# An RWKV attention block and a SwiGLU block in one kernel: weight checks moved to the result buffers, gates made due sooner, last stores on two queues

## The chip, the cores and the metric

The kernel runs on one core of a Trainium2 chip. The metric is the device time of one execution in microseconds. A core has five engines that work side by side and each take their own instructions in order: TensorE (PE, matrix products; PEld is its weight load), VectorE (DVE), ScalarE (ACT), GpSimd (POOL) and SyncE (SP), which here issues the DMA transfers. Engines wait for one another through semaphores.

## The reference

Two blocks follow each other, in float32, with the weights of the second given as float64.

```python
# attention: r, k, v are (B, H, S, D) = (4, 8, 768, 48)
for t in range(S):
    cur = einsum('bhd,bhe->bhde', u * k[t], v[t])
    y[t] = einsum('bhd,bhde->bhe', r[t], state + cur)
    state = w * state + einsum('bhd,bhe->bhde', k[t], v[t])
# bridge: y becomes x, 3072 tokens by 384
xn = x / sqrt(mean(x * x) + 1e-6) * rms_g
out = (silu(xn @ w_gate) * (xn @ w_val)) @ w_out      # 384 -> 1536 -> 384
```

## The kernel before

**Stages.** The sequence is cut into 12 chunks of 64 positions; one chunk of all four batches is 256 tokens. For each chunk, `mixing` (line 735) does the attention: decayed products of r and k (A), a masked diagonal, the outputs (Y), the squares of the outputs into the tile `sq` (line 679), a root mean square (r, sqrt), the scaled tokens xa and xb (a copy with the halves exchanged), and the new state (U, E). `move` is a DMA of some heads' rows.

**The second block.** Chunks 0 and 1 are done in the plain way: cells `g` (gate and value of one group of 128 hidden units) and `P` (output product). During these first 150 us the float64 weights arrive as raw words and are rounded to float32 by VectorE (`bits1`, `bits2`), ScalarE (`ulp`) and GpSimd (`sum`). From chunk 2 on, chunks are taken in pairs (2 and 3, 4 and 5, to 10 and 11), and the two-by-two product of two halves of the weights by two chunks is made with seven products in place of eight. `group` (line 1028) does this for one of six groups of hidden units: products f1 to f7 of twelve matmuls each in the PSUM banks a, b and c, the copy `m1` of bank a on ScalarE, sums g1, g2, g3 on VectorE, Silu on ScalarE (silu0, silu1, silu23), and the gated units h0, h1, h2, h3. f1 and f5 both go into bank a: m1 is copied between them, silu0 and h0 read it after f5. `second_layer` (line 1065) makes the output product of the pair in the same way: P1 to P7, four results (c11 in r0, c12 in r1, c21 in r2, c22 in r3), which lie in `rows_out` (line 313) and are stored by `result` (line 1090), two DMAs of 64 rows each. In the last pair P3, c12 and the store of r1 are split in two halves.

**The checks.** The rounding is exact only for weights whose magnitude is not tiny. `check` (line 713) looks at one of 36 parts of the weights: SP loads 384 KB of raw words from HBM, ScalarE takes Abs of their high words and then a Relu that counts into a column of `seen`. `some_checks` (line 729) adds five of them in the mixing of each chunk from chunk 2 on, until all are done; all use the place `sq`, one after the other. `flag` (line 1133) sums `seen` at the end, and every engine reads the one number `bad` into a register (line 1149); a general path in the program follows if it is not zero.

**What sets the order.** All this is recorded as operations of a `Plan` with an engine, an assumed cost, and keys that are read and written; keys give the dependences. `schedule` (line 128) gives each operation a due time, taken backwards from the goals of the TensorE operations along the dependences, and then lets each free engine take the ready operation that is due first. `search` (line 204) tries 2000 changes of the goals from each of four seeds for the stretch up to the first product of chunk 4. The instructions are then issued in the order of the planned starts, so each engine's order is fixed when the program is built. All of them carry the line 92 in the profile, that of the wrapper that issues them.

```python
for j, hop in self.then[i]:
    due = late[j] - by * (hop + cost)
    ...
    if due < late[i]:
        late[i] = due
```

A load's entry has its cost and `land`, the assumed time until its data can be read: `LAND` is 2.1.

Of the kernel before, what the change touches and what calls it, by code (L numbers as in the profile page):

```python
# [43 lines left out]
I64 = mybir.dt.int64  # L44
# [19 lines left out]
L = 64  # L64
# [30 lines left out]
class Plan:  # L95
# [3 lines left out]
    HOP = 0.2  # L99
    SWITCH = 0.15  # L100
    AHEAD = 30.0
    KEEP = 2.0

    def __init__(self):
        self.ops, self.then, self.last, self.readers = [], [], {}, {}

    def add(self, engine, cost, reads, writes, give, land=0.0, port=False, name="", rows=False):

# [19 lines left out]
    def schedule(self, goals, free, count, relaxed, patience=0.3):  # L128

        if len(self.then) < len(self.ops):
            self.then = [[] for _ in self.ops]
            for i, op in enumerate(self.ops):
                for d in op[2]:
                    self.then[d].append((i, self.hop(d, i)))
        late = [goals.get(i, 1e6 + i) for i in range(len(self.ops))]
        early = min(goals[i] for i in goals if i >= relaxed) - self.AHEAD
        for i in reversed(range(len(self.ops))):
            by, cost = 2 if i >= relaxed else 1, self.ops[i][1]  # L140
            for j, hop in self.then[i]:
                due = late[j] - by * (hop + cost)
                if i < relaxed <= j and due < early:
                    due = early
                if due < late[i]:
                    late[i] = due
        n, then = count, self.then
        free, port = dict(free), {"DVE": 0.0, "POOL": 0.0}
        missing, mode = [len(op[2]) for op in self.ops[0:n]], None
        at, ready, start, end = [0.0] * n, {e: set() for e in free}, [0.0] * n, [0.0] * n  # L150
        for i in range(n):
            if not missing[i]:
                ready[self.ops[i][0]].add(i)
        for _ in range(n):
            when, e = min((max(free[e], min(at[i] for i in ready[e])), e) for e in free if ready[e])
            turn = (lambda i: late[i] + self.KEEP * (self.ops[i][7] != mode)) if e == "PE" else late.__getitem__
            i = min((i for i in ready[e] if at[i] <= when), key=turn)
            sooner = [j for j in ready[e] if at[j] <= when + patience and turn(j) < turn(i) - 1]
            if sooner:
                i = min(sooner, key=turn)  # L160
            s = max(when, at[i])
            if e == "PE":
                s += self.SWITCH * (self.ops[i][7] != mode)
                mode = self.ops[i][7]
            if self.ops[i][5]:
                s = max(s, port["POOL" if e == "DVE" else "DVE"])
            ready[e].remove(i)
            start[i], end[i] = s, s + self.ops[i][1]
            free[e] = end[i]
            if self.ops[i][5]:  # L170
                port[e] = end[i]
            for j, hop in then[i]:
                if j < n:
                    at[j] = max(at[j], end[i] + hop)
                    missing[j] -= 1
                    if not missing[j]:
                        ready[self.ops[j][0]].add(j)
        return start
# [58 lines left out]
def fast(ctx, tc, chan, tok, vpad, wka, wkb, wot, cols, u_row, out, bad):  # L237
# [444 lines left out]
    rms = diag.rearrange("p h t -> p (h t)")  # L682
    ku = raws.tile([P, B, HP, L], FP32, name="ku")
    ms = c_tile([P, 2, 2], "ms")
    turn = {"at": 0, "gv": 0, "h": 0}

    def next_at():
        turn["at"] += 1
# [23 lines left out]

    def check(n, src, k):

        keys = ["sq0", "sq1"]
        raw = sq.bitcast(I64).rearrange("p i t -> p (i t)")[:, 0:CHECK]
        hi = raw.bitcast(I32).rearrange("p (n z) -> p n z", z=2)[:, :, 1].bitcast(FP32)
        add(
            "SP", 0.95, [], keys, lambda: sp.dma_start(out=raw, in_=src[:, k * CHECK : (k + 1) * CHECK]), land=LAND,
            name=f"look {n}",  # L720
        )
        add("ACT", 0.57, [], keys, lambda: act.activation(hi, hi, AF.Abs), name=f"look {n}")
        add(
            "ACT", 0.81, [], keys + ["seen"],
            lambda: act.activation(hi, hi, AF.Relu, scale=-(2.0**15), bias=1.0, accum_out=seen[:, n : n + 1]),
            name=f"look {n}",
        )

    def some_checks():

        for n, (src, k) in list(to_check)[0:5]:
            check(n, src, k)
        del to_check[0:5]

    def mixing(s):

# [107 lines left out]
        if brief:  # L844
            for n in (2, 1):
                add(
                    "DVE", 0.15 + 0.27 * n, ["sq1"], ["sq0"],
                    lambda n=n: dve.tensor_add(sq[:, 0:n], sq[:, 0:n], sq[:, n : 2 * n]), port=True, name=f"q {s}",
                )
            add(  # L850
                "PE", 0.45, ["sq0", "sq1"], [key],
                lambda bank=bank: pe.matmul(bank[:, 0:NT], ones, sq[:, 0], start=True, stop=True), name=f"r {s}",
            )
            some_checks()
            add(
                "ACT", 3.1, [key], ["diag"],
                lambda bank=bank: act.activation(rms, bank[:, 0:NT], AF.Sqrt, scale=1.0 / DM, bias=eps), name=f"sqrt {s}",
            )
            add("DVE", 1.75, [], ["diag"], lambda: dve.reciprocal(rms, rms), name=f"inv {s}")
            add("DVE", 0.95, ["diag", "yT0", "yT1"], [f"xa{x}"], lambda: scaled(s, rms, yT), port=True, name=f"x {s}")  # L860
        else:
            for half in range(2):
                add(
                    "PE", 0.9, [f"sq{half}"], [key], lambda bank=bank, half=half: mean_squares(bank, sq, half),
                    name=f"r {s}",
                )
            if quick:
                add("ACT", 0.3, [key], ["ms"], lambda bank=bank: root(bank, ms[:, 0]), name=f"sqrt {s}")
                add("DVE", 0.15, [], ["ms"], lambda: dve.reciprocal(ms[:, 0], ms[:, 0]), name=f"inv {s}")
            else:  # L870
                add(
                    "DVE", 0.15, [key], ["ms"],
                    lambda bank=bank: dve.tensor_scalar(
                        out=ms[:, 1], in0=bank[:, 2 * P : 2 * P + 2], scalar1=1.0 / DM, scalar2=EPS, op0=ALU.mult,
                        op1=ALU.add,
                    ), name=f"ms {s}",
                )
                add("POOL", 0.6, ["ms"], ["ms'"], lambda: power(ms[:, 0], ms[:, 1]), port=True, name=f"pow {s}")
                add("DVE", 0.35, ["ms'"], ["ms"], lambda: refine(ms[:, 0], ms[:, 1]), name=f"inv {s}")
            add("DVE", 0.4, ["ms"], ["diag"], lambda: on_diagonal(ms[:, 0], diag), port=True, name=f"diag {s}")  # L880
            add("PE", 0.45, ["diag"], [key], lambda bank=bank: spread(bank, diag), name=f"spread {s}")
            add("DVE", 1.0, [key, "yT0", "yT1"], [f"xa{x}"], lambda bank=bank: scaled(s, bank, yT), name=f"x {s}")
# [145 lines left out]
    def group(s, m):  # L1028
# [18 lines left out]
        mm(xs_b, a_keys, a, lambda: wb[i][:, o], lambda: xb[s], False, "f5")  # L1047
        add("ACT", 0.38, ["sums"] + a_keys, ["g0"], lambda: act.activation(late["gv"][:, 0, 0], a[:, 0, 0:NT], AF.Silu), name="silu0")
        add("DVE", 0.42, a_keys + ["g0"], [f"h{m}.0"], lambda: dve.tensor_mul(h[:, 0], a[:, 1, 0:NT], late["gv"][:, 0, 0]), name="h0")
        mm(["t4"], b_keys, b, lambda: wb[i + 2][:, o], lambda: t_of(4), False, "f6")  # L1050
        add("DVE", 0.69, b_keys + ["m1"], ["g2"], lambda: dve.tensor_add(late["gv"][:, :, 2], b[sl], late["m1"]), name="g2")
        add("ACT", 0.62, [], ["g2", "g3"], lambda: act.activation(late["gv"][:, 0, 2:4], late["gv"][:, 0, 2:4], AF.Silu), name="silu23")
# [12 lines left out]
    def second_layer(s):  # L1065
# [22 lines left out]
            line.append(add("PE", 0.325 * len(js) * len(ms), reads, [keys[t]], give, name=f"{name} {s}"))  # L1088

        def result(k, chunk, f, js=(0, 1)):  # L1090
            def give():
                for bl in range(2):
                    to = bass.AP(
                        tensor=out.tensor, offset=out.offset + ((2 * js[0] + bl) * S + chunk * L) * DM + f * HALF,
                        ap=[[DM, L], [2 * S * DM, len(js)], [1, HALF]],
                    )
                    sp.dma_start(out=to, in_=results[bl * L : (bl + 1) * L, k, js[0] : js[-1] + 1])

            add("SP", 1.2, [f"r{k}"], [], give, name="store")

        def plus(writes, reads, to, x, y, name):
            add("DVE", 0.55, reads, writes, lambda: dve.tensor_add(to, x, y() if callable(y) else y), name=name)
# [30 lines left out]
    def flag():  # L1133
# [20 lines left out]
            lambda: pe.matmul(bank[0:1, 0:1], wrong, ones[:, 0:1], start=True, stop=True), name="flag",  # L1154
        )
        add("DVE", 0.2, [key], ["bad"], lambda: dve.tensor_copy(bad, bank[0:1, 0:1]), name="flag")
        add("ACT", 0.6, ["bad"], [], load, name="flag")

    t_sum = lambda s, n, reads, writes: add(
        "DVE", 0.95, reads, writes, lambda: token_sum(s, n), port=True, name=f"t{n} {s}"  # L1160
# [1 line left out]
    for s in range(FIRST, NS, 2):  # L1162
# [4 lines left out]
        t_sum(s, 4, xs_b + ["t2"], ["t4"])  # L1167
        if s == FIRST:
            add("DVE", 1.25, ["wa1.0", "wa1.1"], ["wa3.0", "wa3.1"], lambda: unit_sum(3, 1), port=True, name="sum 3'")
        for m in range(NN // 2):  # L1170
            group(s, m)
        if s == FIRST:
# [495 lines left out]
```

## Time and profile before

| | |
|---|---|
| median of 8 runs | 634.09 us (631.68 to 637.39) |
| profiled execution | 633.27 us |
| its span, first to last instruction | 631.5 us |
| mean granted TensorE clock | 0.995 |
| TensorE busy | 608.9 us, 96% of the span |
| VectorE, ScalarE, GpSimd busy | 437.5, 354.8, 42.8 us |
| HBM read and written | 55.94 MB, 4.72 MB |

The profile is that of one execution. "PE bank_a <- DVE h: 5.0, 3, 2.0" in the list of waits reads: TensorE, before instructions that write bank_a, stood idle for 5.0 us in total, three times, at most 2.0 at once, until an instruction of VectorE that writes h ended. A row of the timeline has start and duration in us, engine, line, operation, what it writes and reads, shapes and a count; in brackets stands the idle time before it and what ended it. A "q" behind an engine's name means its sequencer, which issues DMAs. A window's row has, for each engine, its busy time and number of instructions in the stretch, then the granted clock of TensorE as a share, the share of the DMA engines and GB/s.

### The profile page before, as it was taken

What the parts mean: (1) busy time and instruction counts of PE and PEld (TensorE: products, weight loads), DVE (VectorE), ACT (ScalarE), POOL (GpSimd) and SP (SyncE); (2) the same over time, 40 slices, a digit from 0 to 9 for tenths busy, and PEclk for the clock granted to TensorE, in tenths of its full rate; (3) what the DMA queues carried; (4) which work ended last, traced back from release to release, by engine and by line L of the source; (5) the groups of instructions that cost most, each with busy time, mean ns of one, the idle gap of its engine ahead of it and who ended that gap; (6) DMA issues with size and microseconds to landing.
All of it is one profiled execution on the core that took longest, in us unless ns stands there. A gap on an engine that the chain in (4) does not pass through costs nothing.

```text
span 631.5 us, 15364 instructions
## 1 busy us (share of the span) xinstructions
PE 608.9 (96%) x6544; PEld 538.4 (85%) x6544; DVE 437.5 (69%) x621; ACT 354.8 (56%) x895; POOL 42.8 (7%) x41
## 2 busy tenths in 40 slices
PE   8979999999999999999999899999999989999994
PEld 8867787777788899888899788899888889988994
DVE  7788788887776896477785468695556866455631
ACT  6888578675388447538958438948222774212200
POOL 2245323100000000000000000000000000000000
PEclk9998999999999999999999999999999999999999
DMA  8686763305404414142523242332104011100001
GB/s 283 215 324 205 251 220 120 109 14 176 144 7 125 153 33 100 51 153 67 144 85 97 76 150 60 110 118 57 26 1 152 12 31 32 26 1 2 1 13 44
DMA packets 22782, 62.92 MB, mean 100 GB/s; under 512 B 3152, under 2 KB 10160, under 8 KB 21296
## 3 DMA queue, kind: packets, MB, share of 16 engines
q1 hardware_dynamic: 22704, 61.85, 31.8%
q8 instruction: 53, 0.87, 0.6%
q14 instruction: 25, 0.20, 0.1%
HBM read 55.94 MB, written 4.72 MB: 96 GB/s over the span
## 4 chain that ended last, share of the span: by engine, by line
PE 88%; DMA 4%; ACT 3%; DVE 2%; SPq 1%; issue 1%; ACTq 0%
PE bank_b L92 28%; PE bank_a L92 26%; PE bank_c L92 23%; PE at L92 10%; DMA sq<-in_wka_dram 1%; DMA sq<-in_wot_dram 1%; DMA TOK<-in_tok_dram 1%; ACT L92 1%; SPq L92 1%; DMA VS<-in_vpad_dram 1%; ACT VS L92 1%; ACT sq L92 1%; DVE h L92 1%; DVE rows_out L92 1%; ACT MO L92 0%
## 5 line engine op out<-in xcount | busy, mean ns | idle before, releaser
L92 DVE TENSOR_TENSOR gv<-bank_b,m 128x512 f32<-128x512 f32 x90 | 62.1, 690 | 66.8 <-PE bank_b L92 64.7
L92 PE MATMUL bank_b<-xa,wa 64*128 64x256 f32 x444 | 55.0, 380 | 0.0
L92 ACT ACTIVATE sq<-sq 128x384 f32<-128x384 f32 x72 | 40.2, 559 | 24.1 <-DMA sq<-in_wot_dram 9.8
L92 ACT ACTIVATE gv<-gv 128x512 f32<-128x512 f32 (+1 forms) x60 | 31.1, 522 | 38.9 <-DVE gv L92 38.7
L92 PE MATMUL bank_a<-xa,wa 64*128 64x256 f32 x396 | 49.5, 382 | 3.0 <-DVE h L92 3.0
L92 PE MATMUL bank_a<-wo,h 128*128 128x192 f32 (+1 forms) x264 | 49.4, 343 | 2.0 <-DVE h L92 2.0
L92 ACT ACTIVATE gv<-bank_a 128x256 f32<-128x256 f32 x30 | 11.5, 382 | 70.0 <-PE bank_a L92 69.7
L92 DVE TENSOR_TENSOR gv<-bank_c,gv 128x512 f32<-128x512 f32 x60 | 41.4, 690 | 12.3 <-PE bank_c L92 11.1
L92 PEld LDWEIGHTS bank_a<-wo,h 128*128 128x128 f32 x264 | 43.5, 190 | 6.2 <-DVE h L92 2.1
L92 PE MATMUL bank_a<-xb,wb 64*128 64x256 f32 x396 | 48.7, 378 | 0.0
L92 ACT ACTIVATE ME<-dmask,du 64x64 f32<-64x64 f32 x176 | 45.8, 331 | 4.0 <-DVE du L92 3.3
L92 PEld LDWEIGHTS bank_b<-xa,wa 64*128 64x128 f32 x444 | 42.1, 187 | 6.4 <-issue 1.4
L92 ACT ACTIVATE MO<-dmask,du 64x64 f32<-64x64 f32 x176 | 46.5, 337 | 1.1 <-DVE du L92 0.7
L92 PE MATMUL bank_b<-t,wb 64*128 64x256 f32 x360 | 44.7, 381 | 1.2 <-DVE gv L92 1.2
L92 PEld LDWEIGHTS bank_a<-xa,wa 64*128 64x128 f32 x396 | 37.2, 187 | 9.8 <-DVE h L92 3.8
L92 PE MATMUL bank_c<-t,s 64*128 64x256 f32 x360 | 44.1, 377 | 0.0
L92 PE MATMUL bank_b<-t,s 64*128 64x256 f32 x360 | 44.0, 377 | 0.0
L92 PE MATMUL bank_c<-xb,s 64*128 64x256 f32 x360 | 43.9, 376 | 0.0
L92 ACT COPY m<-bank_a 128x512 f32<-128x512 f32 (+1 forms) x35 | 19.9, 569 | 40.2 <-PE bank_a L92 37.7
L92 PEld LDWEIGHTS bank_a<-xb,wb 64*128 64x128 f32 x396 | 38.0, 187 | 5.0 <-issue 0.5
L92 PE MATMUL bank_b<-wo,h 128*128 128x192 f32 (+1 forms) x168 | 38.4, 385 | 2.6 <-DVE h L92 2.6
L92 PEld LDWEIGHTS bank_b<-t,wb 64*128 64x128 f32 x360 | 34.2, 187 | 5.7 <-DVE gv L92 1.6
(152 smaller groups left out, 1253.2 us busy)
## 6 DMA issues: line engine op xcount, KB each, us to landing
chan<-in_chan_dram SPq DMA_DIRECT2D x11, 1024.0 KB, 5.5
TOK<-in_tok_dram SPq DMA_DIRECT2D x11, 768.0 KB, 5.8
VS<-in_vpad_dram SPq DMA_DIRECT2D x24, 256.0 KB, 4.2
raw<-in_wot_dram SPq DMA_DIRECT2D x8, 576.0 KB, 5.3
sq<-in_wka_dram SPq DMA_DIRECT2D x12, 384.0 KB, 3.3
sq<-in_wkb_dram SPq DMA_DIRECT2D x12, 384.0 KB, 3.1
sq<-in_wot_dram SPq DMA_DIRECT2D x12, 384.0 KB, 3.2
out_dram<-rows_out SPq DMA_DIRECT2D x46, 96.0 KB, 2.3
```

What stands on the lines that cost most here:

```text
L92: return lambda *args, **kwargs: self.tc.keep_in_program_order(give(*args, **kwargs))
```

## The change

The checks use `rows_out` in place of `sq`, its two halves (r0 and r1, r2 and r3) in turn, and their loads are assumed to land in 2 x 2.1 us. They are added in front of the six groups of a pair, eight to a pair, instead of in the mixing. The operation that makes h0 of every group gets a due time 3 us sooner, which passes on to all that it depends on. In the last pair the stores of r2 and r3 are issued from ScalarE's queue. All stores write a key, `stored`, that the reading of the flag reads.

```diff
     AHEAD = 30.0
+    URGENT = 3
...
+            if i in self.urgent:
+                late[i] -= self.URGENT
...
     def check(n, src, k):
-        keys = ["sq0", "sq1"]
-        raw = sq.bitcast(I64).rearrange("p i t -> p (i t)")[:, 0:CHECK]
+        turn["look"] = 1 - turn["look"]
+        keys = [f"r{2 * turn['look'] + i}" for i in range(2)]
+        raw = rows_out[:, turn["look"]].bitcast(I64).rearrange("p j f -> p (j f)")[:, 0:CHECK]
...
-            "SP", 0.95, [], keys, lambda: sp.dma_start(out=raw, in_=src[:, k * CHECK : (k + 1) * CHECK]), land=LAND,
+            "SP", 0.95, [], keys, lambda: sp.dma_start(out=raw, in_=src[:, k * CHECK : (k + 1) * CHECK]), land=2 * LAND,
...
     def some_checks():
-        for n, (src, k) in list(to_check)[0:5]:
+        share = -(-len(parts) // (NS // 2 - 1))
+        for n, (src, k) in to_check[0:share]:
             check(n, src, k)
-        del to_check[0:5]
+        del to_check[0:share]
...
     def mixing(s):
-            some_checks()
...
     def group(s, m):
         add("DVE", 0.42, a_keys + ["g0"], [f"h{m}.0"], lambda: dve.tensor_mul(h[:, 0], a[:, 1, 0:NT], late["gv"][:, 0, 0]), name="h0")
+        if m >= 0:
+            p.urgent.add(len(p.ops) - 1)
...
         def result(k, chunk, f, js=(0, 1)):
+            queue, issue = ("ACT", act) if k > 1 and s + 2 == NS else ("SP", sp)
...
-                    sp.dma_start(out=to, in_=results[bl * L : (bl + 1) * L, k, js[0] : js[-1] + 1])
-            add("SP", 1.2, [f"r{k}"], [], give, name="store")
+                    issue.dma_start(out=to, in_=results[bl * L : (bl + 1) * L, k, js[0] : js[-1] + 1])
+            add(queue, 1.2, [f"r{k}"], ["stored"], give, name="store")
...
     def flag():
-        add("ACT", 0.6, ["bad"], [], load, name="flag")
+        add("ACT", 0.6, ["bad", "stored"], [], load, name="flag")
...
     for s in range(FIRST, NS, 2):
+        some_checks()
         for m in range(NN // 2):
             group(s, m)
```

More of the change, by code (lines that the diff above doesn't have):

```diff
@@ L101 @@
     AHEAD = 30.0
+    URGENT = 3
     KEEP = 2.0
     def __init__(self):
-        self.ops, self.then, self.last, self.readers = [], [], {}, {}
+        self.ops, self.then, self.last, self.readers, self.urgent = [], [], {}, {}, set()
     def add(self, engine, cost, reads, writes, give, land=0.0, port=False, name="", rows=False):
@@ L684, in fast @@
     ms = c_tile([P, 2, 2], "ms")
-    turn = {"at": 0, "gv": 0, "h": 0}
+    turn = {"at": 0, "gv": 0, "h": 0, "look": 0}
     def next_at():
```

## The prediction

> **What bounds the kernel now.** I read the page's busy shares first, then TensorE's own waits, and then went to the place of each wait.
>
> ```profile
> PE 608.9 (96%) x6544; PEld 538.4 (85%) x6544; DVE 437.5 (69%) x621; ACT 354.8 (56%) x895; POOL 42.8 (7%) x41
> PEclk9998999999999999999999999999999999999999
> ```
>
> TensorE is busy for 608.9 of 631.5 us. The change adds and removes no matmul, so all it can move is the 22.6 us in which TensorE stands still, the 0.2 us lost when it changes between row modes (1.50 against 1.29 us for one set of twelve matmuls in the chain), and the dips of its clock. The waits of TensorE over the whole run:
>
> ```profile
> PE bank_a L92 <- DVE h L92: 5.0, 3, 2.0
> PE bank_b L92 <- DVE h L92: 2.6, 1, 2.6
> PE bank_c L92 <- POOL wa L92: 2.3, 1, 2.3
> ...
> PE bank_b L92 <- DVE gv L92: 1.2, 1, 1.2
> ...
> PE bank_c L92 <- DVE bad L92: 0.8, 1, 0.8
> ```
>
> By time, the ends are: 2.27 at 33.7 (POOL's weight sum), 2.56 at 45.5 (first output product P 0 0 waits for h), 1.25 at 163.0, 0.98 at 257.5, 2.03 at 354.4, 2.00 at 508.4 (output product P1 of the pair at chunk 8 waits for the last h0), and 0.80 at 620.9. After the last matmul 7.6 us follow. In the windows around the two early waits the fields after the span are PE, PEld, DVE, ACT, POOL, then the granted clock:
>
> ```profile
> 33.60:36.00 2.40, 0.14 (x4) 0.08 (x2) 2.34 (x5) 2.36 (x5) 2.09 (x3) 1.00 0.51 92
> 45.40:48.00 2.60, 0.06 (x1) 0.01 (x1) 2.25 (x6) 2.58 (x5) 1.83 (x2) 1.00 0.97 307
> 48.50:51.70 3.20, 3.20 (x6) 1.66 (x5) 3.06 (x9) 3.20 (x11) 1.72 (x2) 0.50 0.75 253
> ```
>
> So the wait at 45.5 costs twice: after it the clock is 0.50 for 3.2 us, and P 0 0 takes 5.64 us (48.02 to 53.66) where the same twelve take 3.91 elsewhere. That is 1.73 more. Now ScalarE and the SP queue around 354:
>
> ```profile
> 352.97 1.14 ACT L92 ACTIVATE sq<-sq 128x384 f32<-128x384 f32 x2 [4.67 <-DMA sq<-in_wka_dram]
> 354.21 1.28 ACT L92 ACT_TABLE_LOAD   x1
> 355.51 0.38 ACT L92 ACTIVATE gv<-bank_a 128x256 f32<-128x256 f32 x1
> ```
>
> A weight check stands in ScalarE's order ahead of the Silu of the unit group. Its load was issued at 348.88, behind four stores on SP, and came late; ScalarE stood 4.67 us, then loaded its table, then made silu0, and only then could VectorE make h0, for which TensorE waited 2.03. The waits at 257.5 (ScalarE idle 1.46 for a check's load) and 163.0 (5.72 and 3.29) have the same form. Checks follow one another through one place, sq, so a late load is late for the next one too.
>
> **The change part by part.** The sum is made against the profiled execution, 633.27 us, which is 0.82 under the median of 634.09.
>
> *Checks.* 36 checks stay: 36 loads of 384 KB and 72 activations (0.56 each, plus 36 read-outs of 0.19), about 47 us of ScalarE before and after. In the changed order they stand in pairs inside the first four unit groups of each pair of chunks (8, 8, 8, 8, 4), with two places in turn, and the scheduler assumes 4.2 instead of 2.1 us from the load to ScalarE. The load itself:
>
> ```profile
> DMA to landing us min/median/max: 3.0/3.2/7.3
> ```
>
> What must fit is store, then check, then ScalarE. The places are now rows_out, so a check's load waits on SP until the stores of the results have landed (2.3 median), and SP's next store queues behind it. Let f1 of a pair's first group start at T, when P3 (3.90) ends. By VectorE's order c22 is done about 1.5 earlier; with two issues of 0.6 its store lands at about T+1.6, and the even check, issued then, at T+4.8. The store of r1 (c12, after P3) queues behind that issue, is issued to T+3.3 and lands at T+5.0; the odd check lands at T+8.2. ScalarE has the even check behind silu0, until about T+6.4, and then stands to T+8.2. It makes 1.31 us of check, 0.63 of silu23 and 0.42 of silu1 and is free for the next m1 at T+10.6. The next f1 ends at T+10.4 (eight products of 1.295), and f5 wants m1 (0.58) at T+11.7: the late load is covered, by 0.5. So the three waits, 4.26 together, go; I leave 1.0 for loads above the median. Ends: none left, or all 4.26 again.
>
> *h0 made due 3 us sooner.* In 25 of 30 groups f5 now stands third among TensorE's seven products, ahead of f4 and f3; before it was fifth in 22. h0 is then ready about two products (2.6 us) earlier, which covers the 1.28 table load. P1 at chunk 8 waited 2.00 because h0 of the last group came last on VectorE; I leave 0.2. What is late next is m1: f5 adds to the bank that m1 is copied from. The nearest rows are one undisturbed group:
>
> ```profile
> 549.72 1.46 PE L92 MATMUL bank_a<-xa,wa 64*128 64x256 f32 x12
> 551.02 1.46 PE L92 MATMUL bank_b<-t,s 64*128 64x256 f32 x12
> 551.29 0.58 ACT L92 COPY m<-bank_a 128x512 f32<-128x512 f32 x1 [0.21 <-PE bank_a L92]
> 552.31 1.46 PE L92 MATMUL bank_c<-t,s 64*128 64x256 f32 x12
> ```
>
> m1 ends at 551.87, and the third product starts at 552.31: 0.44 of room, of which a handover takes 0.07 (the last product starts at 621.69, 0.07 after c12 ended at 621.62). So f5 costs nothing where ScalarE is free. In the groups beside mixing ScalarE may hold m1 behind a diagonal (1.05 for four); there are about two such places per pair, and I charge 1.0 in all. Ends: 0, and 0.4 in each of 30 groups, 12 us.
>
> *The first 150 us.* The due times and the checks' new places change the searched order. P 0 0 now stands behind a gate group, with h made before: the 2.56 and the 1.73 of clock go. New narrow places: a gate group behind VectorE's weight rounding (one pair of bits rows is 1.47), and the first f1 of chunk 2, which has only a root product (about 0.6 with its mode change) between it and the product whose h it follows (1.11 from product to h in the group above), so 0.5. I charge 2.0 for all of these; ends 0 and 4.3, as much as goes. The wait at 33.7 stays. TensorE changes row mode 69 times instead of 65: four times 0.20, 0.8.
>
> [...] The 2.56 wait was followed by a clock of 0.50, while those of 2.27, 2.03 and 2.00 were not. [...]
>
> *Last stores.*
>
> ```profile
> 623.93 0.36 DVE L92 TENSOR_TENSOR rows_out<-bank_c,rows_out 128x192 f32<-128x192 f32 x1 [2.26 <-PE bank_c L92]
> 623.95 2.87 SPq L92 DMA_DIRECT2D out_dram<-rows_out  x4
> ```
>
> The last result is ready at 624.29, but its two stores are issued third and fourth of these four, from 625.42, because SP read the flag (780 ns, from 622.7) and then had the two stores of the result's first half. With r2 and r3 on ScalarE's queue, those two go out by about 622.9 and the flag is read by 624.2. The flag does not reach the end on SP: in the changed order it still stands ahead of the last two stores, so a late flag would hold them. Issue at 624.3 instead of 625.42 gives 1.1, and 1.2 with less queued at the landing. Ends: 0 (an issue on ScalarE, which no row shows, as slow as to hold the end) and 2.0. At the wait of 0.80 nothing changes.
>
> The sum: -4.26 +1.0 -2.00 +0.2 +1.0 -2.56 -1.73 +2.0 +0.8 -1.2 = -6.75. From 633.27 this is 626.5.
>
> **The rivals.**
> 1. *Waits only change place.* The searched order and the pairs' order have as many narrow spots as before: new waits of 4.3 early, 4.26 at the checks; then -6.75 +2.3 +3.3 = -1.2, 632.1, no change. For it: every stall here comes from an in-order queue whose order has been redone. Against it: the room of 0.4 at the odd check and 2.6 at h0.
> 2. *Slower: m1 becomes TensorE's gate.* Third place for f5 ties TensorE to ScalarE in 25 to 30 groups. If ScalarE hands m1 over 0.77 later than in the row above, each group loses 0.4, 12 us, and the time is 638.5. It decides from 0.29 lost per group (8.6 us, which is 6.75 and the 1.9 that tell a difference). For it: a check of 1.31 or four diagonals of 1.05 ahead of m1 would do it. Against it: in the order m1 mostly stands before the check in a group, and ScalarE is busy only 56%.
> 3. *Half of it.* The clock dips after the wait at 33.7 instead (1.73 back) and the early waits are 1.5 more: 629.7, still faster.
>
> **How the numbers follow.** Forecast with its half-way rival 3: 0.82. Rival 1: 0.09. Rival 2: 0.09. A measurement of this kernel can tell about 0.3%, 1.9 us. The range: the lower end takes the ends of the unknown costs that can well meet, no early waits (-2.0), none at checks and m1 (-2.0), 0.8 more at the end: 621.7. The upper end passes rival 3 and goes on to 631.5, just short of rival 1; above it lies about 0.15, below the range 0.04. Faster by over 0.3%: 0.82; within: 0.09; slower: 0.09.
>
> **What would show it.** Right: the wait of P 0 0 and the 0.5 clock at 48 gone; ScalarE's waits for check loads (22.6 us now) halved; no wait of bank_a for h at a pair's second group or at P1; end minus last matmul about 6.4 us instead of 7.6. Wrong: TensorE waiting for ScalarE's m many times; the odd check of a pair landing after T+9; a wait above 2.5 us before 60 us with a clock of 0.5 after it; the last store issued after the flag on SP.

## The result, and the profile after

The changed kernel takes 637.83 us (median of 12 runs, 635.38 to 641.64), the kernel before 634.25 in runs on the same chip (33 runs). The ratio is 1.006, with a 95% interval of 1.0043 to 1.0077: slower by 0.6%, where 1.1% faster was forecast. The profiled execution took 638.48 us with a span of 636.7, so 5.1 more in the span than before (636.66 against 631.54). The busy shares of the changed kernel:

```profile
PE 613.1 (96%) x6536; PEld 540.3 (85%) x6536; DVE 441.2 (69%) x621; ACT 352.4 (55%) x895; POOL 43.6 (7%) x41
```

TensorE is busy 4.2 us longer with the same matmuls (6536 records against 6544: some are missing). Its waits, in the changed kernel:

```profile
PE bank_a L92 <- ACT m L92: 8.9, 4, 2.6
PE bank_c L92 <- POOL wa L92: 3.0, 1, 3.0
...
PE bank_a L92 <- DVE h L92: 0.3, 1, 0.3
```

The first line is new. Four times f5 waits for m1: 1.60 at 249.6, 2.48 at 356.2, 2.23 at 456.2 and 2.60 at 556.0, once in each pair from chunk 4 on. The waits for h (7.6 in two lines before) are down to 0.3, and the wait for POOL is 2.96 where it was 2.27. The windows of the changed kernel around the two early places, and behind the waits at 356.2 and 456.2 (the clock is the number after POOL's):

```profile
36.70:40.00 3.30, 3.30 (x22) 2.30 (x24) 3.27 (x3) 2.90 (x4) 2.95 (x2) 0.50 0.95 324
45.40:48.00 2.60, 2.60 (x25) 2.17 (x21) 1.51 (x3) 2.32 (x7) 0.00 (x1) 1.00 0.14 41
358.80:362.50 3.70, 3.70 (x22) 3.05 (x24) 1.27 (x3) 1.94 (x6) 0.00 (x0) 0.61 0.22 87
...
458.50:462.50 4.00, 4.00 (x22) 3.27 (x24) 1.31 (x3) 1.54 (x5) 0.00 (x0) 0.57 0.25 87
```

At 45.4 TensorE now works through at full clock: the wait of P 0 0 and its dip are gone. But the clock is 0.50 after the wait at 33.7, and 0.61 and 0.57 after those at 356.2 and 456.2: three dips where there was one. None follows the wait of 2.60 at 556.0 (1.00 from 558.6 to 562.1).

By stage, from the start of one pair's P1 to that of the next, from chunk 2 on: before 96.84, 97.90, 97.62 and 84.73; after 97.83, 99.99, 99.74 and 87.60. The first 216 us became 1.71 shorter, the four pairs 8.07 longer, and the time behind the last matmul 1.24 shorter (6.41 against 7.65). That makes the 5.1.

One late wait, followed back, in the changed kernel. Here T is 344.31, where f1 of the pair's first group starts, right behind P3 (the first of these rows, which ends at 344.38):

```profile
340.32 4.06 PE L92 MATMUL bank_c<-wo,h 128*128 128x192 f32 x24
344.31 1.57 PE L92 MATMUL bank_a<-xa,wa 64*128 64x256 f32 x12
```

SP:

```profile
345.47 1.25 SPq L92 DMA_DIRECT2D out_dram<-rows_out  x2
348.51 0.33 SPq L92 DMA_DIRECT2D rows_out<-in_wot_dram  x1
348.94 2.25 SPq L92 DMA_DIRECT2D out_dram<-rows_out  x2
352.94 0.33 SPq L92 DMA_DIRECT2D rows_out<-in_wot_dram  x1
```

The even check's load goes out at T+4.2 and the odd one's at T+8.6; the prediction had T+1.6 and T+5.0. (The expectations below were written with a T some 0.1 to 0.2 later, so T+4.0 there.) ScalarE, and then TensorE:

```profile
352.11 1.14 ACT L92 ACTIVATE rows_out<-rows_out 128x384 f32<-128x384 f32 x2 [3.20 <-DMA rows_out<-in_wot_dram]
...
356.17 1.11 ACT L92 ACTIVATE rows_out<-rows_out 128x384 f32<-128x384 f32 x2 [2.84 <-DMA rows_out<-in_wot_dram]
...
358.11 0.56 ACT L92 COPY m<-bank_a 128x512 f32<-128x512 f32 x1
```

```profile
358.72 1.24 PE L92 MATMUL bank_a<-xb,wb 64*128 64x256 f32 x8 [2.48 <-ACT m L92]
```

The odd check reaches ScalarE at T+11.9, so m1 of the second group starts at T+13.8 and f5 at T+14.4, 2.5 late. (An odd check after T+9 was one of the signs that the prediction named for being wrong.) What held the even check on SP were the stores ahead of it, and they waited for VectorE. VectorE's row in the changed kernel, and then the same row of the kernel before, with P3 of that kernel ahead of it:

```profile
344.42 1.02 DVE L92 TENSOR_TENSOR rows_out<-bank_c,rows_out 128x384 f32<-128x384 f32 x2 [3.39 <-PE bank_c L92]
```

```profile
341.04 4.06 PE L92 MATMUL bank_c<-wo,h 128*128 128x192 f32 x24
345.14 1.02 DVE L92 TENSOR_TENSOR rows_out<-bank_c,rows_out 128x384 f32<-128x384 f32 x2 [4.17 <-PE bank_c L92]
```

These two additions are u4 and c22. Both read the first half of bank_c, which P5 had finished writing 3.9 us before in both kernels (its rows end at 340.48 and 341.20). They start when P3 ends, in both kernels, and P3 writes only the second half; each half is 512 float32 columns of the tile (line 675 of the kernel before). The reading is that P3 stands ahead of them in the order in which the program is issued, and that the wait is made for the tile, not for the half; the experiments test it. The planner has a key for each half (c0, c1), and so does not see this wait.

### The profile page after: what moved, and what is told of

Read it like the earlier page. It is cut to its first block, busy times and chain, and to the rows that moved or that the text cites. A ratio compares the mean times of both kernels' runs of the same rounds, so it can differ in the third digit from the quotient of the medians.

```text
span 636.7 us, 15332 instructions
## 1 busy us (share of the span) xinstructions
PE 613.1 (96%) x6536; PEld 540.3 (85%) x6536; DVE 441.2 (69%) x621; ACT 352.4 (55%) x895; POOL 43.6 (7%) x41
## 4 chain that ended last, share of the span: by engine, by line
PE 89%; DMA 3%; DVE 2%; ACT 1%; issue 1%; POOL 0%; SPq 0%; ACTq 0%; POOLq 0%; DVEq 0%
PE bank_b L92 30%; PE bank_a L92 26%; PE bank_c L92 23%; PE at L92 11%; DMA rows_out<-in_wot_dram 1%; DMA chan<-in_chan_dram 1%; DMA out_dram<-rows_out 1%; ACT rows_out L92 1%; DMA raw<-in_wot_dram 1%; DVE ME L92 0%; ACT gv L92 0%; DVE bits L92 0%; ACT m L92 0%; DVE chan L92 0%; DVE rows_out L92 0%
## 5 line engine op out<-in xcount | busy, mean ns | idle before, releaser
L92 DVE TENSOR_TENSOR gv<-bank_b,m 128x512 f32<-128x512 f32 x90 | 62.1, 690 | 48.8 <-PE bank_b L92 45.2
L92 PE MATMUL bank_a<-xb,wb 64*128 64x256 f32 x396 | 50.9, 391 | 8.9 <-ACT m L92 8.9
L92 DVE TENSOR_TENSOR gv<-bank_c,gv 128x512 f32<-128x512 f32 x60 | 41.5, 691 | 24.3 <-PE bank_c L92 24.0
L92 ACT ACTIVATE gv<-gv 128x512 f32<-128x512 f32 (+1 forms) x60 | 30.6, 521 | 49.2 <-DVE gv L92 49.1
L92 PE MATMUL bank_b<-xa,wa 64*128 64x256 f32 x444 | 56.1, 386 | 0.0
L92 ACT ACTIVATE rows_out<-rows_out 128x384 f32<-128x384 f32 x72 | 39.7, 553 | 25.2 <-DMA rows_out<-in_wot_dram 9.5
L92 PEld LDWEIGHTS bank_a<-xb,wb 64*128 64x128 f32 x396 | 38.5, 191 | 15.8 <-ACT m L92 10.8
L92 ACT ACTIVATE ME<-dmask,du 64x64 f32<-64x64 f32 x176 | 46.0, 331 | 7.6 <-DVE du L92 6.9
L92 PEld LDWEIGHTS bank_b<-xa,wa 64*128 64x128 f32 x444 | 44.1, 193 | 6.5 <-ACT MO L92 0.5
L92 PE MATMUL bank_a<-wo,h 128*128 128x192 f32 (+1 forms) x264 | 49.3, 343 | 0.0
L92 PE MATMUL bank_a<-xa,wa 64*128 64x256 f32 x396 | 49.0, 380 | 0.0
L92 ACT ACTIVATE MO<-dmask,du 64x64 f32<-64x64 f32 x176 | 46.6, 337 | 2.1 <-DVE du L92 1.3
L92 PEld LDWEIGHTS bank_a<-wo,h 128*128 128x128 f32 x264 | 43.6, 190 | 3.8 <-issue 0.3
L92 ACT COPY m<-bank_a 128x512 f32<-128x512 f32 (+1 forms) x35 | 19.9, 567 | 46.9 <-PE bank_a L92 31.8
L92 PE MATMUL bank_b<-t,wb 64*128 64x256 f32 x360 | 45.1, 383 | 0.0
L92 PE MATMUL bank_c<-t,s 64*128 64x256 f32 x360 | 44.3, 378 | 0.0
L92 PE MATMUL bank_b<-t,s 64*128 64x256 f32 x360 | 44.3, 378 | 0.0
L92 PE MATMUL bank_c<-xb,s 64*128 64x256 f32 x360 | 43.9, 376 | 0.0
L92 DVE TENSOR_TENSOR h<-gv 128x512 f32<-128x512 f32 (+1 forms) x60 | 31.2, 553 | 16.6 <-ACT gv L92 16.6
L92 PEld LDWEIGHTS bank_a<-xa,wa 64*128 64x128 f32 x396 | 37.7, 187 | 5.6 <-issue 1.4
L92 PEld LDWEIGHTS bank_c<-t,s 64*128 64x128 f32 x360 | 34.7, 188 | 5.2 <-issue 0.7
L92 PEld LDWEIGHTS bank_c<-xb,s 64*128 64x128 f32 x360 | 34.8, 187 | 4.0
```

What stands on the lines that cost most here:

```text
L92: return lambda *args, **kwargs: self.tc.keep_in_program_order(give(*args, **kwargs))
```

## The experiments

**Theory A:** u4 and c22 are held by P3 through the tile bank_c; that holds the stores, the stores hold the checks' loads, a late check holds m1, and m1 holds f5. The main rival: f5 as third product is too early for ScalarE by itself (the prediction's rival 2; theory B in the expectations). In all these kernels the goals that the search finds for the first 150 us are written into the program as constants (those of the kernel that is the base), so that an edit late in the program leaves the order of that stretch as it was. Ratios are to the kernel before on the same chip.

### P3 in a free half of bank_b

```diff
-keys = {..., "v": "c1"}
+keys = {..., "v": "b1" if s + 2 < NS else "c1"}
-            plus(["r1"], ["c1"], to, x, to, "c12")
+            plus(["r1"], [keys["v"]], to, x, to, "c12")
```

> P3 of the pairs before the last writes half of bank b instead of half of bank c; nothing else is changed against the changed kernel (637.8 us), the order of the first 150 us is kept as it was. Theory A (the sums u4 and c22 on VectorE wait for the end of P3, because P3 was given to TensorE first and writes the same tile bank_c; so the stores, the two checks behind them, ScalarE's m1 and TensorE's f5 are late): the waits of bank_a for m (8.9 us, four times) go, with the clock dips behind them; even check issued about 1.6 us after the first f1 of a pair instead of 4.0; 627 us, 625 to 630. Theory B (f5 as third product makes m1 the gate by itself): the waits of bank_a for m stay at 6 to 9 us, 637 us. Theory C (the loss is in the newly searched first 150 us): 637 us, pairs unchanged.

Measured: 625.38 us (5 runs), ratio 0.986 (0.982 to 0.989). All waits for m are gone. But the planner, told of the new half, also moved a store on SP: the one of r1 now stood ahead of the even check. So the run fitted theory A without showing the wait by itself. The next run does.

### The same with every instruction in its place

```diff
+if s + 2 < NS:
+    bank["v"] = bank_of["b"][:, 1]     # the key stays "c1"
```

> The changed kernel with every instruction in its planned place, but P3 of all pairs before the last writes the free half of bank_b instead of the second half of bank_c; the planner still counts it as bank_c. In the run where the planner knew of the move it also put the store of r1 ahead of the even check, so that run did not show the wait by itself. Theory A (u4 and c22 wait for P3 through the tile bank_c, and this holds the stores, the checks, m1 and f5): u4 starts about 4 us earlier against the start of f1, the even check is issued at T+1.6 to 2.5 instead of T+4.0, TensorE's waits for m at chunks 4, 6, 8 and 10 (1.6, 2.5, 2.2, 2.6) are gone, and the time is 625 to 628, ratio to the kernel before 0.984 to 0.991. Rival (the planner's other order of the SP queue did it): the waits for m stay at 2.0 or more in the last three pairs and the time is 635 to 638.

Measured: 625.09 us (4 runs), ratio 0.986 (0.9833 to 0.9887). TensorE's only wait of over 1.2 us in this kernel:

```profile
PE bank_c L92 <- POOL wa L92: 3.0, 1, 3.0
```

VectorE and ScalarE of this kernel in the same pair, T being 342.26:

```profile
338.90 1.01 DVE L92 TENSOR_TENSOR rows_out<-bank_c,rows_out 128x384 f32<-128x384 f32 x2
```

```profile
350.71 1.15 ACT L92 ACTIVATE rows_out<-rows_out 128x384 f32<-128x384 f32 x2 [2.73 <-DMA rows_out<-in_wot_dram]
...
352.94 0.59 ACT L92 COPY m<-bank_a 128x512 f32<-128x512 f32 x1 [0.15 <-PE bank_a L92]
```

u4 and c22 run straight behind the work ahead of them, at T-3.4 instead of T+0.1. SP issues the even check at 342.99 (T+0.7) and the odd one at 346.86 (T+4.6). ScalarE still waits for the odd check, but has it at T+8.5, and m1 then waits 0.15 for the matmuls of f1: the load is covered. The output of one product was moved and 12.7 us went. Theory A holds, and the other order of SP is not needed for it.

### The checks left out

```diff
-act.activation(hi, hi, AF.Abs)
-sp.dma_start(out=raw, in_=src[:, k * CHECK : (k + 1) * CHECK])
-act.activation(hi, hi, AF.Relu, ..., accum_out=seen[:, n : n + 1])
+None                                   # three times; order kept
+dve.memset(seen, 0.0)
```

> The 36 checks are left out (their loads and activations are not issued, the column they count into is set to zero), all other instructions stand in the changed kernel's order. Theory A: the three waits of bank_a for m in the pairs at chunks 6, 8 and 10 (7.3 us) go; the one of 1.6 us in the pair at chunk 4 stays, since there m1 stands behind a copy of mixing that waits for VectorE behind u4, without a check; 629 us, 627 to 632. Theory B: the waits stay, 635 to 638 us. Theory C: no change in the first 150 us, so 637 us.

Measured: 626.35 us (5 runs), ratio 0.9872 (0.9835 to 0.9909), a little under theory A's 627. One wait of the four stays:

```profile
PE bank_a L92 <- ACT m L92: 1.6, 1, 1.6
```

It is that of the pair at chunk 4, where no check stands between: there u4, held by P3 (3.34 in the changed kernel), delays the product of up and chan on VectorE, ScalarE copies the tile MO of the mixing from it (1.04), and m1 stands behind that copy. The three waits of 2.2 to 2.6 came through the checks.

### The checks behind the first group

```diff
-        some_checks()
         for m in range(NN // 2):
             group(s, m)
+            if m == 0:
+                some_checks()
...
-            "SP", 0.95, [], keys, lambda: sp.dma_start(out=raw, ...
+            "SP", 0.95, ["h0.0"], keys, lambda: sp.dma_start(out=raw, ...
```

> The changed kernel with P3 left in bank_c, so that u4 and c22 still wait for P3 and the stores still go out late, but with each pair's checks added behind its first unit group and loaded only when that group's h0 is made. If the held u4 costs only through the checks (the stores hold the check's load, the load holds m1): the waits for m of 2.2 to 2.6 at chunks 6, 8 and 10 are gone although u4 still starts at T+0.0, the wait of 1.6 at chunk 4 stays, since no check stands in it, and the time is 627 to 630, ratio to the kernel before 0.988 to 0.993. If ScalarE's checks ahead of m1 cost wherever they stand in the first groups: waits for m of 1 us or more appear in the second or third group instead, and the time is 633 to 637.

Measured: 626.94 us (6 runs), ratio 0.9868 (0.9835 to 0.990): the first case, just under its range. VectorE in this kernel:

```profile
344.78 1.02 DVE L92 TENSOR_TENSOR rows_out<-bank_c,rows_out 128x384 f32<-128x384 f32 x2 [3.39 <-PE bank_c L92]
```

u4 is held as long as in the changed kernel, and the only wait for m is the 1.60 of chunk 4. So the held stores cost only where something near waits for them. Thirty-six checks of 1.31 us ahead of ScalarE's other work cost nothing visible when their loads are in time: with no checks at all the ratio was 0.9872.

### The gates not due sooner

```diff
-    URGENT = 3
+    URGENT = 0
```

> The 3 us by which h0's due time was moved are set to 0; checks, places and stores as in the changed kernel, and the searched goals of the first 150 us kept. Theory A: the checks' loads are as late as before, so ScalarE still stands in front of m1 and TensorE waits for g1 or h instead of m1; h0 comes last again, and P1 waits for it about 2 us in three pairs; 637 to 642 us. Theory B: the waits of bank_a for m go and the pairs take what they took in the kernel before; 631 to 634 us. Theory C: 637 us.

Measured: 643.57 us (5 runs), ratio 1.0133 (1.0096 to 1.0171): slower than any of the expectations, with theory A's waits. TensorE's first wait in this kernel:

```profile
PE bank_a L92 <- DVE h L92: 11.8, 8, 2.0
```

Without the due times the move of the checks makes the kernel slower still; with f5 late, h0 comes late eight times. That f5 as third product is by itself the loss is excluded: taking it away costs 4.6 us by the ratios (1.0133 against 1.006).

### The due times alone

The lines with `urgent` from the change, on the kernel before; checks and last stores as they were.

> The kernel before with one part of the change alone: the gate h0 of every unit group due 3 us sooner. Checks and last stores stay as before. If this part is a gain by itself: the wait of 2.00 at P1 of chunk 8 goes, f5 stands third in most groups, and the waits for late checks (1.25, 0.98, 2.03) stay or move to m of the same groups; 631 to 633, ratio 0.994 to 0.998. If it only pays together with the checks' move, since f5 third then meets m1 held by a check in sq: new waits of bank_a for m of over 1 us in two or more pairs, and 634 to 638, ratio 0.999 or more.

Measured: 630.63 us (9 runs), ratio 0.9948 (0.9928 to 0.9968). The first case: the part is a gain by itself. P1 at chunk 8 no longer waits, no wait stands near 354, and m1 is late once, by 1.3. This is at 250.9, where four diagonal operations (1.05) stand ahead of m1; they had waited 2.96 for VectorE, which had itself been held 2.48 by P3 at u4. So this wait, too, may come from the held additions; that was not tested. The wait of P 0 0 was 3.27 here with the clock at 0.50 behind it; nothing was changed in that stretch's order.

### The last stores alone

The new `result` and the flag's `stored`, on the kernel before.

> The kernel before with the last change alone: stores of r2 and r3 of the last pair from ScalarE's queue, flag read ordered behind the stores. All theories: from the last matmul to the end 6.4 us instead of 7.6, so 633.0 against 634.2 (0.998); all else as before.

Measured: 633.12 us (11 runs), ratio 0.9977 (0.9948 to 1.0005): not told apart from no change by time. In the profile, 6.50 us lie behind the last matmul instead of 7.65.

### P3 in bank_b, in the kernel before

The first edit above, on the kernel before.

> The kernel before with P3 of all pairs before the last in the free half of bank_b. If the wait of u4 for bank_c also cost the kernel before: the stores, and with them the check's load behind them on SP at 348.9, are issued 2 to 4 us earlier, TensorE's waits of 0.98 at 257.5 and 2.03 at 354.4 shrink to under 0.5 each, and the time is 630 to 632.5, ratio 0.993 to 0.997. The wait at P1 of chunk 8 goes as well if the planner's shifted order covers it (another 2.0). If the kernel before had slack for the late stores: 633 to 636, ratio 0.998 to 1.002.

Measured: 626.41 us (5 runs), ratio 0.9877 (0.9853 to 0.9901): more than was expected. The waits of 0.98, 2.03 and 2.00 are all gone. From P1 to P1 the pairs take 95.60, 95.59, 95.55 and 84.73, where they took 96.84, 97.90, 97.62 and 84.73. A pair of 95.55 is an undisturbed one: it is found here, in the changed kernel with P3 moved and the order kept, and in the one without checks alike. But the planner was told, and ordered the pairs anew. So the same was run with every instruction in its place:

> The kernel before with P3 of all pairs before the last in the free half of bank_b and every instruction in its planned place (the planner still counts it as bank_c), to part the held stores from the planner's other order in the run where it was told. If the three waits of the pairs (0.98 at 257.5, 2.03 at 354.4, 2.00 at 508.4) all came from u4 held by P3: all are gone, the pairs take 95.6 each, and the time is 626 to 628, ratio 0.986 to 0.990. If only the two in which a late check stands did, and h0 of the last group is late in the plan itself: the 2.00 at P1 of chunk 8 stays, the other two are gone, and the time is 628 to 630, ratio 0.990 to 0.994.

Measured: 630.98 us (12 runs), ratio 0.994 (0.992 to 0.9961). The second case: 0.98 and 2.03 are gone, and the wait at P1 of chunk 8 stays, with 2.00. The pairs take 95.59, 95.84, 97.63 and 86.41. The last is 1.68 over its 84.73, since the 2.00 was followed here by a clock of 0.66 from 507 to 512; without that the time would be about 629.3, inside the expected range. So the held stores cost the kernel before its two waits for late checks. The run with the planner told was another 4.57 faster by the medians (on two chips; 4.0 by the ratios); 3.76 of that lies, in the profiles, in the last two pairs (97.63 + 86.41 against 95.55 + 84.73), where the planner's other order took the wait for h0 away, and the dip with it.

### The wait for POOL filled

```diff
-        if until < 27:
+        if until < 40:
```

This is on top of the first edit; the condition bounds where products of ones are put into TensorE's free time.

> The changed kernel with P3 in bank_b (planner told), and twelve more idle products of ones with ones, 2 and 10, on TensorE ahead of the gate that waits for POOL's weight sum at 33.9; they write a bank half that is not in use and are read by nobody. Theory D (the gap of 2.96 halves the clock for 3.4 us afterwards): the gap falls to under 1.0, the clock from 36.9 to 40.3 is 0.9 or more instead of 0.51, and the time is 1.5 to 1.9 under the run with P3 in bank_b alone (625.4), so 623.5 to 624.0. Rival (the dip comes from what is run then, not from the gap): the dip stays and the time stays within 0.7 of 625.4.

Measured: 623.98 us (5 runs), ratio 0.983 (0.9807 to 0.9853), the lowest median of this study. Windows of these two kernels from 37.0 to 40.5, first with P3 in bank_b alone, then with the wait filled:

```profile
37.00:40.50 3.50, 3.50 (x28) 2.53 (x30) 3.47 (x4) 2.85 (x4) 2.91 (x2) 0.52 0.89 341
```

```profile
37.00:40.50 3.50, 3.50 (x50) 2.96 (x50) 3.40 (x5) 3.44 (x6) 2.74 (x3) 1.00 0.86 320
```

From the start of the gate behind the wait to the next gate it is 5.13 us in the first and 3.51 in the second: the dip costs 1.62. By the medians 1.4 of it are gained, but these come from two chips, and the ratios (0.986 and 0.983) have overlapping intervals. In the profiles the span is only 0.7 shorter, since the filled kernel has a dip of its own earlier, from 20.8 to 27.6, and reaches the gate 1.32 later (38.23 against 36.91):

```profile
22.00:24.00 2.00, 2.00 (x12) 2.00 (x11) 1.96 (x5) 1.36 (x4) 0.00 (x0) 0.50 0.05 12
```

No gap of TensorE over 0.8 us stands in the 15 us before that dip. So the dip behind the wait went with the gap, in one place, as theory D has it; but a gap is not the only thing that a dip can follow.

## Why the prediction was wrong

**The step that failed** is the sentence "By VectorE's order c22 is done about 1.5 earlier". It took the order of VectorE's instructions for their times and did not look at the idle time in front of them. The row with `[4.17 <-PE bank_c L92]` stood in the trace of before. With the true start, T+0.1, the store of r3 is issued to T+2.4 and the even check only at T+4.2; the odd check reaches ScalarE 3.7 later than worked out (T+11.9 for T+8.2), and the cover was 0.5. The excess of 3.2 lies above the 2.2 to 2.6 measured, in part because m1 followed the odd check by 1.9 and not by the 2.4 worked out. With the held start removed, the rest of the working came out: odd check at T+8.5 for T+8.2, next m1 at T+10.7 for T+10.6, no wait. Some of that closeness is luck: the two loads left 0.9 and 0.4 earlier than worked out, and the odd one took 3.9 from its issue to ScalarE in place of 3.2.

**Its price.** For the checks the forecast was -4.26 +1.0, and m1 +1.0. In their place came waits for m of 7.3 in three pairs, 1.6 in the first, and two dips. A dip costs 1.96 there: the pair from chunk 4 to 6 took 99.99, which is 4.44 above the undisturbed 95.55, and 2.48 of it is the wait. The forecast charged late m1 with its wait alone; the clock after it was not in the sum, though the profile had a clock of 0.50 behind the wait at 45.5.

**Right in size.** The wait of P 0 0 and its dip at 48 went. The wait at P1 of chunk 8 went. The end became 1.24 shorter (1.2 forecast). The copy of MO ahead of m1 in the pair at chunk 4 cost 1.6, where 1.0 was charged for ScalarE's work around the mixing; here the size was right by luck, since this wait too came through the held u4 and is gone with P3 moved.

**Wrong in size.** The wait at 33.7 was to stay as it was; it grew by 0.69, and the dip came behind it, as rival 3 had it. The gate there took 2.93 us where twelve such matmuls take 1.57. With this, P1 of chunk 2 starts 1.71 earlier, not the 3.3 that the early terms of the sum and the check at 163.0 make (2.56 + 1.73 + 1.25 - 2.0 is 3.5, less a share of the mode changes). Of the 0.8 for mode changes nothing is to be seen: TensorE is busy 608.6 us with the checks behind the first group and 608.9 before, with one dip each, and 609.1 with P3 moved and the order kept, with two.

**The rivals.** The outcome looks like rival 2, m1 as TensorE's gate, and the sign is its sign. But its mechanism, a loss in each of 25 to 30 groups from f5 as third product, is not what happened: four groups of thirty waited, and without the early f5 the kernel is slower.

**What the change is worth.** With P3 out of the way and each order kept, the kernel before stands at 0.994 and the changed one at 0.986 of the time before: the change gains 0.8%, some 5 us (0.008 of 634), where 6.75 were forecast. The hold costs the kernel before 3.8 (634.82 to 630.98) and the changed one 12.7 (637.83 to 625.09), mostly since the checks now stand right behind the held stores (with no checks, 11.5 of it are gone). That difference of 8.9 turned the forecast's sign. The planner, told of the new place, also reaches 0.9877 without the change, where it reaches 0.986 with it; the intervals (0.9853 to 0.9901 and 0.982 to 0.989) overlap, so in that setting no gain of the change is shown.

## What to carry to other kernels

An order of instructions gives no times: before an end is worked out from "it stands ahead of that", read the bracket of its own row, what it waits for and whether it reads what that releaser writes. A wait for a product that writes the other half of the same tile was not needed here, and a planner with finer keys than the program's tiles hid it; a move of that product's output to another tile, all else in place, both tested and mended it. When several waits of different engines come once per stage, look for one late producer behind all of them before pricing each.

## What was not expected of the hardware

For gaps of TensorE of 2.0 to 2.6 us the length did not tell whether a lower clock followed. In the kernel before, the wait of 2.56 was followed by a clock of 0.50, those of 2.27, 2.03 and 2.00 by 1.00 (in the windows from 36.7 to 40.0, 354.4 to 358.0 and 510.0 to 514.0). The gap of 2.96 at 33.7 was followed by a clock of 0.50 to 0.68, from 37.0 to 40.5, in each of the six profiles that have it, the gaps of 2.48 and 2.23 in the changed kernel by 0.61 and 0.57, but the one of 2.60 at 556.0 by 1.00 (from 558.6 to 562.1). With P3 moved in the kernel before and its order kept, the same 2.27 and 2.00 were followed by 0.60 (from 36.7 to 40.0) and 0.66 (from 507 to 512). In four profiles the clock was also at 0.50 from 22 to 24 us, with no gap over 1.2 us in the ten us before: the last stores alone, the due times alone, P3 moved with the order kept, and the wait filled. Why a gap of 2.0 to 2.6 was followed by a dip in one run and by none in another was not shown, and what led to the four dips without a long gap stays open. A dip cost 1.62, 1.68 and 1.96 us in the places worked out above, behind gaps of 2.96, 2.00 and 2.48.

A pair of stores that SP issues in 1.25 us took 2.25 at 348.94, right behind the issue of a 384 KB load; at 343.42 in the kernel with the order kept it took 1.25 behind the same load. What made the difference stays open.
